# Retention and a snake feed-forward in one kernel: six 128-token tiles moved from wide TensorE tiles to 64x64 ones

## The chip, the cores and the metric

One core of a Trainium2 chip runs the kernel. The metric is the device time of one execution in microseconds (us), the median of several runs. Engines are named as in the profile: PE (TensorE, matmuls), PEld (its weight loads), DVE (VectorE), ACT (ScalarE), POOL (GpSimd), SP (SyncE). L12 is line 12 of the kernel before.

## The reference, cut to what matters

```python
# retention: B, H, S, D = 4, 8, 768, 64, token by token
state = gamma[None, :, None, None] * state + np.einsum('bhd,bhe->bhde', k[:, :, t], v[:, :, t])
y[:, :, t] = scale * np.einsum('bhd,bhde->bhe', q[:, :, t], state)
# feed-forward on x: the y of all heads side by side, [3072, 512]; w_in [512, 2048], w_out [2048, 512]
h = x @ w_in
s = np.sin(alpha * h)
g = h + s * s / (alpha + 1e-09)
return (g @ w_out).astype(np.float32)
```

## The kernel before, in words

**Tiles.** The 768 tokens of each of the 4 batches are cut into 6 tiles of 128, 24 in all, number j = 6 * batch + c. `order` (called P from L600 on) gives their sequence: P[0] to P[3] are the first tiles (c = 0) of the four batches, P[4] to P[8] are batch 0 with c = 1 to 5, P[9] and P[10] are batch 1 with c = 1 and 2, and so on. A tile's retention gives 128 columns of `xT`, the transposed input of the feed-forward. The feed-forward works on groups: group 0 is P[0] to P[3] (512 tokens), each later group g is two tiles (256 tokens; group 1 is P[4] and P[5], group 2 is P[6] and P[7]).

**Retention of a tile** has four products: scores (k times q, 128 x 128 for each head, then masked on DVE into `aT`), mix (v times `aT`), inter (the state kept from earlier tiles times q) and sums (k times v, added to the state). Inter and mix add up in PSUM, and the result, multiplied by the decay table `qg`, goes to `xT`: the tile's exit.

There are two forms. The *natural* form (`stage_A`, `stage_M`, `stage_S`, `keep_S`) holds a tile as 128 tokens on partitions. Its scores use 64-row by 128-column tiles of the PE array, its mix and sums 128-row by 64-column tiles, and its state lies as a block diagonal `s_bd`, written by ACT straight from PSUM, where the sums of a batch keep adding up in one bank (`ps`). `stage_M` issues the exit (L327, one DVE instruction) and the state copies (L303) at once. The *wide* form (`inter`, `scores`, `sums`, `mix`, gathered in `burst`) is for P[10] and later; all its matmuls are on 64x64 tiles, four of which work beside one another. A burst finishes the tile `old` while it does the scores of the tile `new`, and it returns three pieces of later work: "exit" (two DVE multiplies, L414), "keep" (two DVE adds into `s_f`, L421) and "hand" (a copy `s_q` <- `s_f`, on ACT for batches 0 to 2, L427). The phase runs these in its next slot.

**The order of the work is the program's order on each engine** (the schedule is manual). After a start with hand-written order, `phase(g, ...)` runs group g in 8 slots, (g,0) to (g,7). A slot issues, in this order: `Slot` (8 matmuls `ph`, L456, then two sines on ACT, L459), the square (L464 on ACT; in slots (1,2) and (1,5) on DVE, L466), the pieces left by the last burst (exit, keep, hand), the retention work put at this slot (`where`: P[6]'s scores at (1,1), the rest of P[6] with P[7]'s scores at (1,3), P[7] with P[8] at (1,6), then slots 1 and 5 of each phase), the mask of those scores, some `po` matmuls of the group before (L481), and `add` (two DVE instructions, L471, that end `gT` and free the `ph` bank). P[4] and P[5] are finished just before phase 1, each between `fill(4)`s, which are four `po` matmuls.

**Loads.** POOL issues all loads of q, k, v, w_in and w_out, in program order. `load_w_in(i)` is one DMA of 512 KB (four of them), L119. q, k and v of a natural tile are DMAs of 128 KB (L84).

**Tables.** `later_tables` (L193) makes `tok`, `lgq` and `expoq` on DVE, ahead of the first mask multiply.

Of the kernel before, what the change touches and what calls it, by code (L numbers as in the profile page):

```python
# [8 lines left out]
F32 = mybir.dt.float32  # L9
# [7 lines left out]
def kernel(  # L17
# [15 lines left out]
    nc = tc.nc  # L33
# [35 lines left out]

    def chunk_of(t, j):  # L70
        b, c = divmod(j, NCH)
        return t[b, :, c * C:(c + 1) * C, :].rearrange("h s d -> s h d")
# [17 lines left out]
    def spot(h):  # L90

        return h // NP, (h % NP) ^ (h // NP)

    def load_seq(bt, names="qkv"):

        cs = [c for c in range(NCH) if wide(bt * NCH + c)]
        nh = 2 * len(cs)
        if "q" in names:
            raw["seq", bt] = (big.tile([128, nh, 2, NP, D], BF16, name=f"qk_seq{bt}"),
                              big.tile([128, nh, NP, D], BF16, name=f"v_seq{bt}"))  # L100
        tqk, tv = raw["seq", bt]
        for name, src in (("q", q), ("k", k), ("v", v)):
            if name not in names:
                continue
            for h in range(H):
                b, at = spot(h)
                r = slice(64 * b, 64 * b + 64)
                o = tv[r, :, at, :] if name == "v" else tqk[r, :, "qk".index(name), at, :]
# [9 lines left out]
    def load_w_in(i):  # L118
        nc.gpsimd.dma_start(out=w_in[:, :, i * fw:(i + 1) * fw], in_=w_in_v[:, :, i * fw:(i + 1) * fw])  # L119
# [62 lines left out]
    for p in range(NP):  # L182
        for e in range(2):
            nc.vector.memset(lgp[64 * e:64 * e + 64, p:p + 1], lng[2 * p + e])
# [41 lines left out]
    s_bd = [big.tile([128, NP, 128], BF16, name=f"s_bd{i}") for i in range(2)]  # L226
# [53 lines left out]
    def stage_S(j):  # L280
        c = j % NCH
        if c == 0:
            st["ps"] = psum.tile([128, NP, D], F32, name="ps", tag="ps")
        ps = st["ps"]
        for p in range(NP):
            for e in range(2):
                nc.tensor.matmul(ps[64 * e:64 * e + 64, p, :], raw["k", j][:, 2 * p + e, :], raw["v", j][:, 2 * p + e, :],
                                 start=(c == 0 and p == 0), stop=True, skip_group_check=True)
        return ps

    def turned(to, ps, copy):

        copy(to[:, 0:2], ps[:, 0:2])
        for e in range(2):
            copy(to[64 * e:64 * e + 64, 2:4], ps[64 - 64 * e:128 - 64 * e, 2:4])

    def keep_S(j, ps):
        if wide(j + 1):
            turned(s_q[(j % NCH + 1) % 2], ps, nc.scalar.copy)
            return  # L300
        for e in range(2):
            r = slice(64 * e, 64 * e + 64)
            nc.scalar.copy(s_bd[(j % NCH + 1) % 2][r, :, r], ps[r, :, :])  # L303

    def stage_M(j):
        c = j % NCH
# [3 lines left out]
        qkT, aT, vs = st["qkT", j], st["aT", j], raw["v", j]  # L310
        py = psum.tile([128, NP, 128], F32, name="py", tag="ty")
        if c > 0:
            for p in range(NP):
                for e in range(2):
                    r = slice(64 * e, 64 * e + 64)
                    nc.tensor.matmul(py[r, p, :], s_bd[c % 2][:, p, r], qkT[:, p, :],
                                     start=(p == 0), stop=True, skip_group_check=True)
        for p in range(NP):
            for e in range(2):
                nc.tensor.matmul(py[64 * e:64 * e + 64, p, :], vs[:, 2 * p + e, :], aT[:, e, p, :],  # L320
                                 start=(c == 0 and p == 0), stop=True, skip_group_check=True)
        x = xT[g][:, :, i * C:(i + 1) * C]
        if c == 0:
            nc.scalar.copy(x, py)
            return
        ps = stage_S(j) if c < NCH - 1 else None
        nc.vector.tensor_mul(x, py, qg[:, c])  # L327
        if ps is not None:
            keep_S(j, ps)

    def half(x):
        return slice(64 * x, 64 * x + 64)
# [3 lines left out]
    def inter(j):  # L338

        qkT, s = st["qkT", j], s_q[j % NCH % 2]  # L340
        st["py", j] = [psum.tile([128, 512], F32, name=f"py{b}", tag=tag) for b, tag in enumerate(("ps", "ty"))]
        for m in range(2):
            for b, e in tiles4:
                last = nc.tensor.matmul(st["py", j][b][half(e ^ b), m * 128:(m + 1) * 128].rearrange("p (f i) -> p f i", f=2),  # L344
                                        s[half(e), 2 * b + m, :], qkT[half(e), m:m + 5:4, half(b)],
                                        start=(m == 0), stop=True, skip_group_check=True)
        return last

    def scores(j):

        qkT = st["qkT", j]
        pa = st["pa", j] = psum.tile([128, 2, 512], F32, name="pa", tag="pa")
        for m in range(2):
# [8 lines left out]
        aT = work.tile([128, 2, 2, 192], BF16, name="aTw", tag="aT", bufs=2)  # L362
        st["aT", j] = aT
# [3 lines left out]
    def sums(now, to, lo):  # L367

        ks, vs = raw["k", now], raw["v", now]
        for f in range(2 if wide(now) else 1):  # L370
            for m in range(2):
                for b, e in tiles4:
                    h = 4 * b + 2 * m + (e ^ b)
# [5 lines left out]
    def mix(j, behind):  # L379

        n = nc.tensor.nop()
        tc.add_manual_dep(n.ins, behind.ins.name, AFTER)
# [7 lines left out]

    def burst(old, new, first=None):

        c = old % NCH
        behind = inter(old)
        more = scores(new) if new is not None else {}
        now = old if c < NCH - 1 else first
        at = None
        if now is old:
# [3 lines left out]
        mix(old, behind)  # L402
        py = st["py", old]
        if now is not None and now is not old:
            at = [py[b][:, 256:384] for b in range(2)]
            sums(now, py, 256)
        g, i = place[old]
        if g not in xT:
            xT[g] = work.tile([128, KS, sizes[g] * C], BF16, name="xT", tag="xT", bufs=3)
        x = xT[g][:, :, i * C:(i + 1) * C]  # L410
# [6 lines left out]
        def keep():  # L417
            for b in range(2):
                o, add = s_f[:, 2 * b:2 * b + 2], at[b].rearrange("p (m d) -> p m d", m=2)
                if wide(now):  # L420
# [179 lines left out]
    def A(j):  # L600
        return lambda: stage_A(j)

    def M(j):
        return lambda: stage_M(j)

    def SK(j):
        return lambda: keep_S(j, stage_S(j))

# [21 lines left out]
    for t in s_bd:  # L630
        nc.vector.memset(t, 0.0)
# [58 lines left out]
    stage_A(P[4])  # L690
# [59 lines left out]
    def into_sum():  # L750
        turned(s_f, st["ps"], nc.vector.tensor_copy)

    def M_last(j):
        stage_M(j)
        into_sum()

# [55 lines left out]
```

## Time and profile before

| | |
|---|---|
| median of 3 runs | 213.49 us (213.29 to 213.51) |
| the profiled execution, its own time | 213.53 us |
| its span (first to last instruction) | 211.7 us |
| PE busy, DVE busy, ACT busy, POOL busy | 94%, 74%, 74%, 50% of the span |
| granted TensorE clock | 1.0 |
| 735 `ph` and 344 `po` matmuls, busy | 98.6 and 90.4 us |

Times in the views are us from the span's start. A row of the timeline or the chain has the start, the length, the engine, the tile or instruction with its line, and how many instructions it merges; in brackets stands how long the engine was idle before and what released it. Rows of PE give start to modelled end, so a matmul's end is later than the start of the next one; a few per cent of its records are missing (344 `po` matmuls are recorded, 368 weight loads for them).

### The profile page before, as it was taken

Reading aid. Unit: us, or ns where it says so; the run is one execution under the profiler, and the core shown is the slowest. Engines: PE = TensorE matmul, PEld = TensorE weight load, DVE = VectorE, ACT = ScalarE, POOL = GpSimd, SP = SyncE. Lnnn points to the kernel's source line nnn. Section 1 sums busy time; section 2 is a strip of 40 time slices with the busy share of each in tenths; the row PEclk is TensorE's granted clock in tenths of the full one; section 3 lists DMA queues with packets and bytes.
Section 4 is the critical chain, followed back from the end, with each engine's and each line's share of the span. In section 5 each row is a group of like instructions: output and inputs, shape, how many; then the busy total and the mean of one; then the engine's idle time right before and its main releaser. Section 6 shows DMA issues by size and latency. Waiting matters only on the chain.

```text
span 211.7 us, 5581 instructions
## 1 busy us (share of the span) xinstructions
PE 199.4 (94%) x2227; PEld 131.0 (62%) x2253; DVE 155.7 (74%) x353; ACT 157.7 (74%) x339; POOL 105.2 (50%) x140
## 2 busy tenths in 40 slices
PE   7798899899989999999999999999999999999994
PEld 3345454457766766766666667666666666666653
DVE  5877849966997688687777787777777878666550
ACT  7588696858887887877867877876876786788821
POOL 8975434977989649699799951001021020000000
PEclk9999999999999999999999999999999999999999
DMA  8999999999997989999999994403513110110112
GB/s 124 154 198 186 206 207 173 154 148 240 142 152 71 166 129 159 113 133 140 140 182 167 193 127 104 99 24 79 88 38 81 54 48 5 50 50 3 50 50 99
DMA packets 101337, 25.00 MB, mean 118 GB/s; under 512 B 93872, under 2 KB 98368, under 8 KB 101312
## 3 DMA queue, kind: packets, MB, share of 16 engines
q0 software_dynamic: 77504, 13.38, 86.7%
q1 hardware_dynamic: 23664, 11.22, 26.3%
q8 instruction: 17, 0.28, 0.6%
q14 instruction: 8, 0.07, 0.1%
q10 hardware_dynamic: 144, 0.07, 0.1%
HBM read 27.27 MB, written 6.29 MB: 159 GB/s over the span
## 4 chain that ended last, share of the span: by engine, by line
PE 78%; DVE 14%; ACT 4%; issue 3%; ACTq 0%
PE po L481 33%; PE ph L456 31%; DVE gT L471 5%; DVE aT L277 4%; PE spare L525 3%; ACT s L459 2%; ACT s L464 2%; PE poh L506 2%; PE py L344 2%; PE py L387 1%; DVE s L466 1%; PE pa L273 1%; PE pa L355 1%; PE py L320 1%; PE pa L374 1%
## 5 line engine op out<-in xcount | busy, mean ns | idle before, releaser
L471 DVE SCALAR_TENSOR_TENSOR gT<-s,rec_alpha,ph 128x256 bf16<-128x256 f32 (+3 forms) x184 | 82.4, 489 | 36.0 <-ACT s L464 35.8
L459 ACT ACTIVATE s<-ph,alpha_sb 128x256 f32<-128x256 f32 (+3 forms) x184 | 79.3, 480 | 35.2 <-PE ph L456 34.5
L456 PE MATMUL ph<-xT,w_in 128*128 128x256 bf16 (+3 forms) x735 | 98.6, 277 | 0.3 <-DVE gT L471 0.2
L481 PE MATMUL po<-w_out,gT 128*128 128x512 bf16 x344 | 90.4, 379 | 4.8 <-issue 3.3
L456 PEld LDWEIGHTS <-w_in 128*128 128x128 bf16 x736 | 70.6, 98 | 30.6 <-issue 1.0
L464 ACT ACTIVATE s<-s 128x512 f32<-128x512 f32 (+1 forms) x92 | 57.1, 621 | 2.5
L481 PEld LDWEIGHTS <-gT 128*128 128x128 bf16 x368 | 33.8, 98 | 27.7 <-issue 1.2
L427 POOL CAST s_q<-s_f 128x256 bf16<-128x256 f32 x5 | 2.0, 397 | 43.3 <-DVE s_f L421 25.7
L143 POOL TENSOR_TENSOR v_seq<-v_seq,kgq 128x512 bf16<-128x512 bf16 x14 | 14.6, 1066 | 8.8 <-ACT s L459 4.9
L109 POOL DMA_DIRECT2D qk_seq<-in_q_dram x24 | 17.1, 743 | 3.2 <-DMA v_seq<-in_v_dram 1.7
L109 POOL DMA_DIRECT2D qk_seq<-in_k_dram x24 | 17.0, 731 | 2.4 <-DMA qk_seq<-in_q_dram 1.3
L109 POOL DMA_DIRECT2D v_seq<-in_v_dram x24 | 17.0, 756 | 0.0
L493 DVE COPY o_sb<-po 128x512 f32<-128x512 f32 x19 | 13.1, 692 | 5.2 <-PE po L481 5.2
L364 DVE TENSOR_TENSOR aTw<-pa,maskq 128x768 bf16<-128x768 f32 x14 | 13.3, 952 | 0.0
L84 POOL DMA_DIRECT2D vr<-in_v_dram x10 | 9.2, 924 | 3.3 <-DMA w_in<-in_moe_w_in_dram 1.7
L525 PE MATMUL spare<-warm 128*128 128x512 bf16 x27 | 9.2, 464 | 1.3 <-DVE warm L162 1.2
L414 DVE TENSOR_TENSOR xT<-py,qg 128x256 bf16<-128x256 f32 x28 | 10.5, 417 | 0.0
L84 POOL DMA_DIRECT2D qkr<-in_q_dram x9 | 8.1, 902 | 3.8 <-DMA w_in<-in_moe_w_in_dram 1.7
L84 POOL DMA_DIRECT2D qkr<-in_k_dram x9 | 8.1, 898 | 3.9 <-DMA w_out<-in_moe_w_out_dram 3.4
L143 POOL TENSOR_TENSOR vr<-vr,kg 128x512 bf16<-128x512 bf16 x7 | 7.4, 1072 | 1.4 <-DMA vr<-in_v_dram 1.4
L277 DVE TENSOR_TENSOR aT<-pa,mask 128x1024 bf16<-128x1024 f32 x6 | 7.3, 1218 | 0.4 <-PE pa L273 0.4
L277 DVE TENSOR_TENSOR aT<-pa,dec 128x1024 bf16<-128x1024 f32 x4 | 4.9, 1223 | 1.8 <-PE pa L273 1.8
(94 smaller groups left out, 141.5 us busy)
## 6 DMA issues: line engine op xcount, KB each, us to landing
out_dram<-o_sb SPq DMA_DIRECT2D x23, 256.0 KB, 2.8
w_in<-in_moe_w_in_dram POOLq DMA_DIRECT2D x4, 512.0 KB, 11.0
w_out<-in_moe_w_out_dram POOLq DMA_DIRECT2D x4, 512.0 KB, 14.8
vr<-in_v_dram POOLq DMA_DIRECT2D x10, 128.0 KB, 6.9
qk_seq<-in_q_dram POOLq DMA_DIRECT2D x16, 80.0 KB, 6.9
qk_seq<-in_k_dram POOLq DMA_DIRECT2D x16, 80.0 KB, 5.1
v_seq<-in_v_dram POOLq DMA_DIRECT2D x16, 80.0 KB, 5.5
qkr<-in_q_dram POOLq DMA_DIRECT2D x9, 128.0 KB, 7.0
```

What stands on the lines that cost most here:

```text
L84: nc.gpsimd.dma_start(out=t, in_=chunk_of(src, j))
L109: nc.gpsimd.dma_start(out=o, in_=src[bt, h, cs[0] * C:, :].rearrange("(f i) d -> i f d", i=64))
L143: eng.tensor_mul(t, t, by[:, j % NCH, :, None].to_broadcast([128, H, D]))
L277: nc.vector.tensor_mul(aT.rearrange("p e n t -> p (e n) t"), pa.rearrange("p e n t -> p (e n) t"), m)
L364: return {"mask": lambda: nc.vector.tensor_mul(aT, pa[:, :, 0:384].rearrange("p e (m t) -> p e m t", m=2), maskq[:, None, None, :].to_broa ...
L456: nc.tensor.matmul(self.ph[:, m, :], w_in[:, i, f * 128:(f + 1) * 128], xT[g][:, i, self.lo:self.hi], start=(m == 0 and i == 0), stop=(i = ...
L459: nc.scalar.activation(out=self.s[:, m, :], in_=self.ph[:, m, :], func=ACTF.Sin, scale=alpha_sb[:, f:f + 1])
L464: nc.scalar.activation(out=self.s, in_=self.s, func=ACTF.Square)
L471: nc.vector.scalar_tensor_tensor(gT[self.g][:, f, self.lo:self.hi], self.s[:, m, :], rec_alpha[:, f:f + 1], self.ph[:, m, :], op0=ALU.mult ...
L481: nc.tensor.matmul(po[g, ts], gT[g][:, f, ts * C:(ts + 1) * C], w_out[:, f, :], start=(f == 0), stop=(f == FF - 1))
L493: nc.vector.tensor_copy(o_sb, po[g, ts])
L525: nc.tensor.matmul(spare["ps"], warm[:, :128], warm, start=True, stop=True)
```

## The change

P[4] to P[9] now go through `scores`, `inter` and `burst` as the wide tiles do, with branches for their natural layout. `s_bd`, its two memsets, `stage_S`, `keep_S`, `turned` and `into_sum` are gone.

- *Scores* of such a tile: 16 matmuls on 64x64 tiles, 128 columns each, in place of 8 on 64x128 tiles. The mask multiply keeps its size.
- *Mix and sums* come in two rounds by token half (`round_of`). In a round each of the four 64x64 tiles takes one half of the tokens: 8 matmuls of mix (4 with 128 columns, 4 with 64) and 8 of sums (64 columns). Both rounds add into the same PSUM places from different halves of the array's rows, so a `nop` on PE waits, after the next tile's scores, until the first round has ended (`behind`).
- *State*: `first_state` copies the first tile's sums to `s_q[1]` (ACT) and `s_f` (DVE); after that keep and hand do it, as in the wide form. Exit, keep and hand are run in the next slot; after P[4] and P[5] they are run at once.
- *Layout*: heads 4 to 7 no longer lie swapped in `load_seq`, in the tables (`lgq` in one copy for each half instead of two, `lgp`) and in `stage_M`'s output; instead w_in's last 256 rows are loaded with their 64-row halves swapped, as three DMAs (256, 128 and 128 KB) for each `load_w_in`.

```diff
 def load_w_in(i):
-    nc.gpsimd.dma_start(out=w_in[:, :, i * fw:(i + 1) * fw], in_=w_in_v[:, :, i * fw:(i + 1) * fw])
+    c = slice(i * fw, (i + 1) * fw)
+    nc.gpsimd.dma_start(out=w_in[:, 0:2, c], in_=w_in_v[:, 0:2, c])
+    for e in range(2):
+        nc.gpsimd.dma_start(out=w_in[half(e), 2:4, c], in_=w_in_v[half(1 - e), 2:4, c])
...
-            for e in range(2):
-                nc.vector.tensor_copy(lgq[r, e::2], lg[r, NP * b + (e ^ b):NP * b + NP:2])
+            nc.vector.tensor_copy(lgq[r], lg[r, NP * b:NP * b + NP])
...
+    def first_state(j):
+        ps = psum.tile([128, NP, D], F32, name="ps", tag="ps")
+        for p in range(NP):
+            for e in range(2):
+                nc.tensor.matmul(ps[half(e), p, :], raw["k", j][:, 2 * p + e, :], raw["v", j][:, 2 * p + e, :],
+                                 start=(p == 0), stop=True, skip_group_check=True)
+        nc.scalar.copy(s_q[1], ps)
+        nc.vector.tensor_copy(s_f, ps)
...
 def scores(j):
+        if not wide(j):
+            for p in range(NP):
+                for f, e in tiles4:
+                    nc.tensor.matmul(pa[half(f), e, 128 * p:128 * p + 128], qkT[half(e), NP + p, half(f)],
+                                     qkT[half(e), p, :], start=(p == 0), stop=True, skip_group_check=True)
...
+    def round_of(j, now, n):
+        py, aT, vs = st["py", j], st["aT", j], raw["v", j]
+        for m in range(2):
+            for b, e in tiles4:
+                f, p = e ^ n, 2 * b + m
+                last = nc.tensor.matmul(py[b][half(e ^ b), m * 128 + 64 * f:(m + 1) * 128], vs[half(f), 2 * p + e, :],
+                                        aT[half(f), e, p, 64 * f:], start=False, stop=True, skip_group_check=True)
+        if now is not None:
+            ks, vs = raw["k", now], raw["v", now]
+            for m in range(2):
+                for b, e in tiles4:
+                    f, h = e ^ b ^ n, 4 * b + 2 * m + e
+                    last = nc.tensor.matmul(py[b][half(e), 256 + 64 * m:320 + 64 * m], ks[half(f), h, :],
+                                            vs[half(f), h, :], start=False, stop=True, skip_group_check=True)
+        return last
 def burst(old, new, first=None):
-        behind = inter(old)
+        now = old if c < NCH - 1 else first
+        last = inter(old)
+        if not wide(old):
+            last = round_of(old, now, 0)
         more = scores(new) if new is not None else {}
...
+        behind(last)
...
+            round_of(old, now, 1)
...
-    stage_A(P[5])
+    scores(P[5])["mask"]()
     fill(2)
-    SK(e0)()
+    first_state(e0)
     scale_v(P[5], nc.vector)
     fill(4)
-    stage_M(P[4])
+    run(burst(P[4], None), "exit", "keep", "hand")
     fill(4)
-    stage_M(P[5])
+    run(burst(P[5], None), "exit", "keep", "hand")
     fill(4)
     where = {6: (1, 1), 7: (1, 3), 8: (1, 6)}
...
-        if n > 6 and wide(P[n - 1]):
+        if n > 6:
             at(where[n], B(P[n - 1], new, first))
         else:
-            if n > 6:
-                at(where[n], lambda j=P[n - 1], last=wide(new): (M_last if last else stage_M)(j))
-            at(where[n], lambda j=new: (scores if wide(j) else stage_A)(j))
-            if first is not None:
-                at(where[n], SK(first))
+            at(where[n], lambda j=new: scores(j))
```

More of the change, by code (lines that the diff above doesn't have):

```diff
@@ L278, in stage_A, with x_of @@
         st["aT", j] = aT
[L280 to L284, printed above, removed]
+    def first_state(j):
+        ps = psum.tile([128, NP, D], F32, name="ps", tag="ps")
         for p in range(NP):
             for e in range(2):
[L287 to L306, printed above, removed]
+                nc.tensor.matmul(ps[half(e), p, :], raw["k", j][:, 2 * p + e, :], raw["v", j][:, 2 * p + e, :],
+                                 start=(p == 0), stop=True, skip_group_check=True)
+        nc.scalar.copy(s_q[1], ps)
+        nc.vector.tensor_copy(s_f, ps)
+    def x_of(j):
         g, i = place[j]
@@ L309, in stage_M @@
             xT[g] = work.tile([128, KS, sizes[g] * C], BF16, name="xT", tag="xT", bufs=3)
-        qkT, aT, vs = st["qkT", j], st["aT", j], raw["v", j]
+        return xT[g][:, :, i * C:(i + 1) * C]
+    def stage_M(j):
+        aT, vs = st["aT", j], raw["v", j]
         py = psum.tile([128, NP, 128], F32, name="py", tag="ty")
[L312 to L317, printed above, removed]
         for p in range(NP):
             for e in range(2):
[L320 to L334, printed above, removed]
+                nc.tensor.matmul(py[half(e ^ (p // 2)), p, :], vs[:, 2 * p + e, :], aT[:, e, p, :],
+                                 start=(p == 0), stop=True, skip_group_check=True)
+        nc.scalar.copy(x_of(j), py)
     tiles4 = [(b, e) for b in range(2) for e in range(2)]
@@ L343, in inter @@
             for b, e in tiles4:
-                last = nc.tensor.matmul(st["py", j][b][half(e ^ b), m * 128:(m + 1) * 128].rearrange("p (f i) -> p f i", f=2),
-                                        s[half(e), 2 * b + m, :], qkT[half(e), m:m + 5:4, half(b)],
-                                        start=(m == 0), stop=True, skip_group_check=True)
+                o, p = st["py", j][b][half(e ^ b), m * 128:(m + 1) * 128], 2 * b + m
+                if wide(j):
+                    o, to = o.rearrange("p (f i) -> p f i", f=2), qkT[half(e), m:m + 5:4, half(b)]
+                else:
+                    to = qkT[half(e), p, :]
+                last = nc.tensor.matmul(o, s[half(e), p, :], to, start=(m == 0), stop=True, skip_group_check=True)
         return last
@@ L401, in burst @@
             sums(now, [pa[:, b] for b in range(2)], 384)
[L402 to L410, printed above, removed]
+        behind(last)
+        if wide(old):
+            mix(old)
+            if now is not None and now is not old:
+                sums(now, py, 256)
+        else:
+            round_of(old, now, 1)
+        x = x_of(old)
         def leave():
@@ L689 @@
     F((0, 1), (12,))
-    stage_A(P[4])
+    scores(P[4])["mask"]()
     a.sq("A").add()
```

46 lines of the change are left out of this document (17 added, 29 removed).

## The prediction

> **What bounds the kernel now.** I read the page first (busy shares, the chain by line), then the chain in order of time, then the timelines of PE, DVE and ACT around the six tiles, then the landings of POOL's DMAs one by one.
>
> ```profile
> PE 199.4 (94%) x2227; PEld 131.0 (62%) x2253; DVE 155.7 (74%) x353; ACT 157.7 (74%) x339; POOL 105.2 (50%) x140
> PE 78%; DVE 14%; ACT 4%; issue 3%; ACTq 0%
> ```
>
> PE bounds most of the span, but the chain's 14% of DVE is not spread out: it lies ahead of 63 us, where the changed tiles are. The chain in order of time, end of phase 1:
>
> ```profile
> 49.62 0.69 DVE qkT L259
> 50.31 0.43 DVE qg L220
> 50.74 0.09 issue
> 50.83 0.86 DVE gT L471 x2
> ...
> 59.67 0.87 DVE gT L471 x2
> 60.55 0.60 DVE xT L327
> 61.15 1.13 DVE aT L277
> 62.28 0.79 DVE gT L471 x2
> 63.07 0.04 issue
> 63.11 1.02 PE po L481 x4
> ```
>
> From 50.83 to 63.07 the chain never leaves DVE: one instruction starts as the one before ends. 60.55 is P[7]'s exit in slot (1,6), 61.15 the mask of P[8], 62.28 the add of slot 6. After 63.11 the chain is PE without a gap to the end, so what happens before it is carried to the end whole, and PE time saved after it counts in full. PE in the same stretch:
>
> ```profile
> 58.91 0.41 PE L316 MATMUL py<-qkT,s_bd 128*64 128x128 bf16 x8
> 59.16 0.39 PE L320 MATMUL py<-aT,vr 128*64 128x128 bf16 x8
> 59.38 0.29 PE L287 MATMUL ps<-vr,qkr 128*64 128x64 bf16 x8
> 59.60 0.40 PE L273 MATMUL pa<-qkT 64*128 64x128 bf16 x8
> 61.68 1.04 PE L456 MATMUL ph<-xT,w_in 128*128 128x256 bf16 x8
> 63.11 1.02 PE L481 MATMUL po<-w_out,gT 128*128 128x512 bf16 x4 [0.40 <-DVE gT L471]
> 63.97 1.04 PE L456 MATMUL ph<-xT,w_in 128*128 128x256 bf16 x8
> ```
>
> 61.68 is slot (2,0): it needs xT of P[7], ready at 61.15. 63.97 is slot (2,1). PE is only 0.56 us ahead of DVE (its 8 `ph` end at 62.55, `po` starts at 63.11).
>
> **The change, part by part.** All against the profiled execution, 213.53 us (span 211.7 and 1.83 around it), 0.04 above the median.
>
> *PE work of a burst.* Groups of four 64x64 matmuls share their time in a wide burst: inter 81.17 to 81.31, 16 scores to 81.48, 16 sums (64 columns) to 81.61, then the mix and on to `po` at 81.89 (the first recorded `po`, 82.11, less one unrecorded of 0.22). So a group costs some 0.053 us at 128 columns, 0.03 at 64. A natural burst then needs inter 0.14, a round 0.16 (0.107 mix, 0.054 sums), scores 0.21 (16 x 128 columns, as long as today's 8 at two abreast), a round and the end 0.28, and 0.10 ahead of it as now: 0.89. Today P[8] with P[9]'s scores and the sums of tile 6 in slot (2,1) takes 64.84 to 66.09, 1.25; P[9] in (2,5) 73.03 to 74.13, 1.10, against 0.88 after. Those lie after 63 us: **-0.58**. The wait of `behind` is covered where scores stand between (0.21 against a matmul's 0.19 and 0.03 of signal). The bursts in (1,3) and (1,6) also save 0.2 each, in a stretch that DVE sets: nothing.
> The Trainium skill (TensorEngine Tiling (Array Packing), Key Properties) says that a change of tiling mode drains TensorE; here the rows of sums and scores (59.38, 59.60) follow at their plain rate, so no price shows. At the 0.1 us in front of a burst for one mode fewer, the two bursts would save 0.2 more.
>
> *P[4] and P[5].* Today ACT copies the state straight from PSUM beside four `po` (45.68 to 46.44) and P[5] starts at 46.53. After the change: burst of P[4] at 44.87 (first_state's DVE copy, between the 0.28 of 128 columns and the 0.69 of 512, is done by 44.8), inter and round 0 to 45.17, an uncovered wait to 45.4, last mix ends 45.7. Then exit, keep and hand follow one another. Their rows in the wide form:
>
> ```profile
> 83.61 0.75 DVE L414 TENSOR_TENSOR xT<-py,qg 128x256 bf16<-128x256 f32 x2
> 84.27 0.47 DVE L421 TENSOR_TENSOR s_f<-s_f,pa 128x128 f32<-128x128 f32 x2
> ```
>
> That is 1.13 from 45.74, to 46.87, then 0.39 of ACT (L427) to 47.3, then P[5]'s inter at 47.38: **+0.85**, PE idle behind four `po` that end by 46.5. P[5]'s burst costs 0.1 more than today's `stage_M` (the uncovered wait), so slot (1,0) starts at 49.05 instead of 48.10. ACT's queue makes it worse: hand (49.4 to 49.8) now stands ahead of the o_sb copy (0.58) and the first sine, which waited for nothing but PE; sine at 50.35 instead of 49.18, so the first add comes at **52.0** instead of 50.83. Bounds: 0 (if the hand-off hid behind `po`) to +1.5.
>
> *DVE in phase 1.* From the first add to P[7]'s old place, 50.83 to 60.55, DVE is packed for 9.72 us. P[6]'s exit of 0.60 becomes exit and keep, 1.06 back to back: 10.18.
>
> *P[7]'s exit moves behind two things.* Today it stands ahead of P[8]'s mask; as a left-over piece it runs in slot (1,7), behind that mask (1.13) and the add of slot 6 (0.79), and takes 0.75: 52.0 + 10.18 + 1.13 + 0.79 + 0.75 = 64.85. Slot (2,0) needs it: 64.9 instead of 61.68. Its `ph` (0.87) and the four `po` (0.86; their wait of 0.56 is gone, that add being done) bring slot (2,1) to 66.63 instead of 63.97: **+2.66**. Hand of P[6] on ACT holds up the sines of slot 5 to 60.35, just ahead of the DVE square that needs them (60.5): nothing more.
>
> *Tables.* Two of four small copies (L201) go. The chain runs through them: tables from 7.10, first mask multiply at 8.70, ten instructions in 1.60 us: 0.16 each, **-0.3**. Bounds 0 and -1.0 (two recorded durations of 0.49). What follows has cover of 0.35 from the landings (w_in's first piece lands at 15.0, used at 15.57). The memsets of s_bd (0.55 at 17.35) lie ahead of 0.60 of DVE idle: nothing.
>
> *Loads.* Eight more DMAs, some 0.75 us each on POOL: 6.0 us. POOL waits there anyway; each issue starts just after the eighth one before it has landed:
>
> ```profile
> 15.35 0.74 POOL L119 DMA_DIRECT2D w_in<-in_moe_w_in_dram  x1 [1.29 <-DMA w_in<-in_moe_w_in_dram]
> 17.87 0.74 POOL L122 DMA_DIRECT2D w_out<-in_moe_w_out_dram  x1 [1.78 <-DMA w_in<-in_moe_w_in_dram]
> 25.50 0.87 POOL L84 DMA_DIRECT2D qkr<-in_q_dram  x1 [1.65 <-DMA w_in<-in_moe_w_in_dram]
> ```
>
> Such waits sum to 13 us between 15 and 36. The landings are paced by bytes, not by issues (one after another 2.5 us for 512 KB, 0.9 for 128 KB, from 12.5 to 43), and with the same eight in flight I get the same landings. Nothing, unless half-height pieces are slower, below.
>
> **Sum:** 2.66 - 0.58 - 0.3 = +1.78: 213.53 + 1.78 = **215.3**.
>
> **Rivals.**
>
> *DVE follows PE (not slower).* Place: DVE from 50.83 to 63.07. If its instructions stand back to back only because PE and ACT release them at that pace, the added keeps and the late exit slip into slack, and only P[5]'s late start and PE's savings are left: 0.95 - 0.4 (the two bursts in phase 1) - 0.58 - 0.3 = -0.33, 213.2. It decides once DVE reaches P[7]'s exit 2.4 us sooner than I reckon, at PE's own arrival (61.68 + 0.95 - 0.4 = 62.2). For it: in the whole kernel DVE's adds wait 35.8 us for ACT. Against it: in this stretch the waits are 0.02 to 0.09, and PE, not DVE, waits at its end. Chance 0.14.
>
> *Half-height loads run at half rate.* Place: the 64-row pieces. Half of each w_in load at twice the time is 1.25 more, 5.0 in all; landings have little slack (P[5]'s k at 40.0, its transposes at 40.1), so nearly all comes through: 213.53 + 1.78 + 4.7 = 220.0. For it: POOL's 64-row loads of 64 KB (L109) moved one each 0.7 us, 94 GB/s, against 152 for 128-row ones. Against: that is POOL's own issue time, not the data's. Chance 0.06.
> The Trainium skill (DMA: Bandwidth & Descriptors, The descriptor swizzle) describes a 128-partition load in which half the engines write partitions 0 to 63 and half the rest, which would be this rival if a 64-row piece kept to its half; the same page's section on how many engines a DMA takes gives 64 rows all sixteen, which would be my case. No row here tells the two apart.
>
> *Otherwise* my mechanism: 0.80.
>
> **The numbers.** My own case reaches from 213.9 (no stall ahead of P[5], -0.7 for the tables) to 216.6 (the tables and the PE savings give nothing, the hand-off at its upper bound). To hold 8 in 10 the range takes in the upper half of the first rival: 213.3 to 216.7. Within 0.2% (0.43 us), about what a measurement of this kernel can tell from no change, lie some 0.10 of the first rival and 0.02 of my case; below it 0.05; slower 0.83.
>
> **What would show it.** After: PE idle some 0.9 us ahead of P[5]'s inter, released by ACT s_q; a PE idle of over 2 us ahead of the `ph` of slot (2,0), released by the DVE xT of L414's counterpart; DVE packed from 52 to 65; the natural bursts of phase 2 at 0.9 us. I am wrong if slot (2,0) starts when PE gets there, if w_in's pieces land later than 15.0, 17.6, 25.3 and 30.4, or if PE waits for DMA before 43 us.

## The result, and the profile after

The changed kernel takes **216.45 us** (median of 4 runs, 215.85 to 217.34) against 213.44 us of the kernel before: a ratio of 1.0145, 95% interval 1.0106 to 1.0184. It is slower, as forecast; the time lies 1.15 us above the forecast of 215.3 and inside its range. The profiled execution is one of the long ones: 217.34 us, span 215.6.

The page of the changed kernel, its busy shares, its row of the granted clock in 40 slices, and the chain by engine:

```profile
PE 201.2 (93%) x2371; PEld 130.8 (61%) x2397; DVE 157.6 (73%) x365; ACT 155.2 (72%) x331; POOL 110.4 (51%) x148
PEclk9999999999996999999999999999999999999999
PE 72%; DMA 12%; DVE 7%; POOL 5%; issue 2%; ACT 0%; POOLq 0%
```

PE is busy for longer though its bursts got shorter: one slice, about 65 to 70 us, ran at a lower clock. DMA and POOL are on the chain now; before, it held neither. The chain in order of time around the late exit:

```profile
52.15 0.87 DVE gT L475 x2
...
61.44 0.87 DVE gT L475 x2
62.32 1.13 DVE aT L334
63.45 0.49 DVE gT L475 x2
63.94 0.20 issue
64.14 0.43 DVE xT L418
64.58 0.04 issue
64.62 1.15 PE ph L460 x8
```

L475 is the add (L471 before), L334 the mask, L418 the exit. From the first add at 52.15, DVE is packed for 10.17 us up to P[8]'s mask (62.32); then come the mask, the add of slot 6 and P[7]'s exit, and slot (2,0) starts when the first half of that exit has ended. PE's timeline there (in brackets its idle time before, and the releaser):

```profile
64.62 1.15 PE L460 MATMUL ph<-xT,w_in 128*128 128x256 bf16 x8 [1.85 <-DVE xT L418]
...
66.98 1.91 PE L460 MATMUL ph<-xT,w_in 128*128 128x256 bf16 x8
```

The first row is slot (2,0), the second slot (2,1). Its eight matmuls take 1.91 us instead of 1.04. Busy times in stretches of 2 us say why; the number after POOL's count is the granted clock:

```profile
62.00:64.00 2.00, 0.77 (x6) 0.34 (x4) 2.00 (x4) 1.47 (x3) 1.06 (x2) 1.00 3.07 151
64.00:66.00 2.00, 1.38 (x10) 0.97 (x10) 2.00 (x7) 0.68 (x2) 1.40 (x3) 0.98 2.39 115
66.00:68.00 2.00, 2.00 (x8) 1.03 (x7) 0.42 (x2) 1.58 (x4) 2.00 (x3) 0.50 0.64 41
68.00:70.00 2.00, 1.97 (x61) 1.42 (x60) 0.71 (x3) 1.04 (x3) 2.00 (x4) 0.66 0.27 55
```

PE has little to do while it waits for DVE (0.77 and 1.38 of 2 us), and then runs at half clock from about 65.9 to 69.3. Nothing in the prediction counted that.

The starts of the feed-forward slots (first matmul of L460, in the profiled execution of each kernel; the forecast's are those that it names, without its -0.3 for the tables; its (2,2) and (2,6) are its (2,1) with the distances of before less the savings that it forecast for the bursts) show where the time goes. From (2,6) on nothing changes: each difference there stands unchanged at the last slot (199.88 before, 203.57 after: 3.69 both times).

| slot | before | forecast | after | exit_first | exit_add_mask | keep_first | hand_later | v_ahead |
|---|---|---|---|---|---|---|---|---|
| (1,0) | 48.10 | 49.05 | 49.34 | 50.22 | 48.93 | 49.56 | 48.57 | 49.07 |
| (1,7) | 60.38 | - | 61.30 | 62.17 | 60.90 | 61.52 | 60.83 | 61.02 |
| (2,0) | 61.68 | 64.9 | 64.62 | 63.57 | 62.39 | 64.84 | 62.33 | 62.44 |
| (2,1) | 63.97 | 66.63 | 66.98 | 67.13 | 65.95 | 66.68 | 64.30 | 64.41 |
| (2,2) | 66.96 | 69.26 | 70.78 | 69.82 | 68.65 | 69.38 | 68.71 | 67.55 |
| (2,6) | 75.00 | 77.08 | 78.69 | 77.73 | 76.56 | 77.29 | 76.61 | 75.46 |

### The profile page after: what moved, and what is told of

It reads as the page before. It is cut to its first block, busy times and chain, and to the rows that moved or that the text cites. A ratio compares the mean times of both kernels' runs of the same rounds, so it can differ in the third digit from the quotient of the medians.

```text
span 215.6 us, 5863 instructions
## 1 busy us (share of the span) xinstructions
PE 201.2 (93%) x2371; PEld 130.8 (61%) x2397; DVE 157.6 (73%) x365; ACT 155.2 (72%) x331; POOL 110.4 (51%) x148
## 4 chain that ended last, share of the span: by engine, by line
PE 72%; DMA 12%; DVE 7%; POOL 5%; issue 2%; ACT 0%; POOLq 0%
PE po L485 32%; PE ph L460 30%; DMA w_in<-in_moe_w_in_dram 7%; DMA qkr<-in_k_dram 5%; DVE gT L475 3%; PE py L321 2%; POOL qkr L87 2%; POOL vr L87 2%; PE poh L510 2%; DVE aT L334 2%; PE py L372 1%; DVE xT L418 1%; PE pa L338 1%; PE pt L253 1%; POOL w_out L123 1%
## 5 line engine op out<-in xcount | busy, mean ns | idle before, releaser
L475 DVE SCALAR_TENSOR_TENSOR gT<-s,rec_alpha,ph 128x256 bf16<-128x256 f32 (+3 forms) x184 | 82.5, 489 | 37.5 <-ACT s L468 37.2
L460 PE MATMUL ph<-xT,w_in 128*128 128x256 bf16 (+3 forms) x735 | 99.9, 279 | 2.6 <-DVE xT L418 1.9
L460 PEld LDWEIGHTS <-w_in 128*128 128x128 bf16 x736 | 70.8, 98 | 34.3 <-issue 4.0
L144 POOL TENSOR_TENSOR v_seq<-v_seq,kgq 128x512 bf16<-128x512 bf16 x14 | 14.6, 1065 | 9.8 <-issue 6.2
L418 DVE TENSOR_TENSOR xT<-py,qg 128x256 bf16<-128x256 f32 x40 | 15.0, 418 | 1.9 <-PE py L389 1.9
L431 ACT CAST s_q<-s_f 128x256 bf16<-128x256 f32 x14 | 5.5, 392 | 6.8 <-DVE s_f L425 6.8
L334 DVE TENSOR_TENSOR aT<-pa,mask 128x1024 bf16<-128x1024 f32 x6 | 7.3, 1222 | 1.9 <-PE pa L331 1.7
L144 POOL TENSOR_TENSOR vr<-vr,kg 128x512 bf16<-128x512 bf16 x7 | 8.0, 1153 | 1.3 <-DMA vr<-in_v_dram 1.3
```

The lines of the kernel that those rows point to most:

```text
L144: eng.tensor_mul(t, t, by[:, j % NCH, :, None].to_broadcast([128, H, D]))
L334: return {"mask": lambda: nc.vector.tensor_mul(aT.rearrange("p e n t -> p (e n) t"), pa.rearrange("p e (n t) -> p (e n) t", n=NP), mask_bc)}
L418: nc.vector.tensor_mul(x[:, 2 * b:2 * b + 2, :], py[b][:, 0:256].rearrange("p (m t) -> p m t", m=2), qg[:, c, 2 * b:2 * b + 2])
L460: nc.tensor.matmul(self.ph[:, m, :], w_in[:, i, f * 128:(f + 1) * 128], xT[g][:, i, self.lo:self.hi], start=(m == 0 and i == 0), stop=(i = ...
L475: nc.vector.scalar_tensor_tensor(gT[self.g][:, f, self.lo:self.hi], self.s[:, m, :], rec_alpha[:, f:f + 1], self.ph[:, m, :], op0=ALU.mult ...
```

## The experiments

The theory: P[7]'s exit, queued on DVE behind P[8]'s mask and the add of slot 6, costs most of it, and P[4]'s exit ahead of its hand-off most of the rest. The rivals: the loads in pieces, and the clock. From one re-ordering to the next the intervals of the ratio overlap, so what a single step does is read from its trace. L numbers from here on are of the changed kernel; "before" on the same chips was 213.48 or 213.49.

**again** and **again2**: the changed kernel, two more times.

> The changed kernel once more, beside the others. Theory: the median comes near 216.3 us; where the granted clock is 1.0 throughout, slot (2,1) starts some 2.4 us later than before (63.97), and the execution takes 215.7 to 216.2; where the clock falls behind the idle time ahead of slot (2,0) it takes 1 to 1.5 us more, so the runs of this kernel scatter over 1 us or more. Rival (the scatter is not of the clock): every run has a clock of 1.0 and they scatter as much.

Measured: 217.35 us (215.76 to 217.69), ratio 1.0161, 1.0122 to 1.0200. The profile repeats the wait: slot (2,0) at 65.05 after 1.90 idle. It also shows one reason why executions of this kernel differ. DVE scales P[5]'s v while POOL scales P[6]'s (both L144). The rows of the first measurement, then those of again:

```profile
44.88 1.60 POOL L144 TENSOR_TENSOR vr<-vr,kg 128x512 bf16<-128x512 bf16 x1 [1.32 <-DMA vr<-in_v_dram]
44.89 0.68 DVE L144 TENSOR_TENSOR vr<-vr,kg 128x512 bf16<-128x512 bf16 x1
```

```profile
44.86 1.04 POOL L144 TENSOR_TENSOR vr<-vr,kg 128x512 bf16<-128x512 bf16 x1 [1.32 <-DMA vr<-in_v_dram]
44.91 1.55 DVE L144 TENSOR_TENSOR vr<-vr,kg 128x512 bf16<-128x512 bf16 x1
```

In every trace of a changed kernel one of the two is long: 1.59 or 1.60 on POOL (1.04 otherwise), or up to 1.56 on DVE (0.68 otherwise). P[4]'s exit, keep and hand stand on DVE and ACT behind DVE's row. So P[5]'s inter comes 2.59 us after P[4]'s where DVE's row is short, and 2.92 to 2.96 where it takes 1.51 to 1.55 (again, again2, exit_first, pe_filled). Before the change rows of 0.96 and 1.38 (before, before_half) made no difference: 1.66 both times.

> The changed kernel a third time, on the chip of pe_filled, to have its executions at a clock of 0.992 counted there: 4 of 10 have shown one, so 2 to 4 of some 6, and a median of 216.3 to 217.4. If none shows one, pe_filled tells nothing of the clock.

Measured: 216.40 us (215.54 to 218.47), ratio 1.0116, 1.0096 to 1.0136. (The expectation miscounts: 5 executions, not 4, of the first 10 had shown a mean clock of 0.991 or 0.992.) The count missed as well: again2 showed one such execution in 6, where 2 to 4 were expected. In all, 6 of 16 did (1 of 4, 4 of 6 and 1 of 6); they average 217.64 us, the other ten 216.23. So a fall of the clock costs some 1.4 us, and the schedule without it costs 2.7.

**exit_first**: in slot (1,6), the exit of P[7] ahead of P[8]'s mask.

```diff
+            if (g, n) == (1, 6):
+                run(fresh, "exit")
             run(fresh, "mask")
```

> In slot (1,6) alone the exit of P[7] is issued before the mask of P[8], as it was before the change. Theory (the late exit holds up slot (2,0), but the add of slot 6, which frees a bank for the po matmuls, is the next limit): slot (2,0) starts at 63.0 instead of 64.6, slot (2,1) only some 0.5 us earlier, since the add of slot 6 now ends at 64.9; TensorE's longest idle is cut in two pieces, so the clock stays at 1.0 and the median falls by 0.5 to 1.2 us against the changed kernel. Rival (the exit alone is the price): slot (2,1) starts 1.5 us or more earlier.

Measured: 215.66 us (215.09 to 217.87), ratio 1.0113, 1.0069 to 1.0156; no execution below a clock of 0.997. PE's timeline:

```profile
63.57 1.15 PE L460 MATMUL ph<-xT,w_in 128*128 128x256 bf16 x8
65.81 1.02 PE L485 MATMUL po<-w_out,gT 128*128 128x512 bf16 x4 [1.09 <-DVE gT L475]
67.13 1.03 PE L460 MATMUL ph<-xT,w_in 128*128 128x256 bf16 x8 [0.29 <-ACT o_sb L499]
```

The wait ahead of slot (2,0) is gone, although this execution began phase 1 late (slot (1,0) at 50.22). But the `po` behind it now wait 1.09 for the add of slot 6, which the mask still holds up, and slot (2,1) waits for ACT. From (1,0) to (2,1) it takes 16.91 us, against 15.87 before. The changed kernel's 17.64 is no fair measure, since its clock fell ahead of (2,1); keep_first and w_whole below hold the same late exit and take 17.12 at full clock. So this step regains some 0.2 of 1.25: the wait has mostly moved.

**exit_add_mask**: exit, add and only then the mask.

```diff
+            late = {}
+            if (g, n) == (1, 6):
+                run(fresh, "exit")
+                late["mask"] = fresh.pop("mask")
             run(fresh, "mask")
...
             now.add()
+            run(late, "mask")
```

> In slot (1,6) alone VectorE's order is exit of P[7], add of slot 6, mask of P[8]; the mask is wanted only in slot (2,1). Theory: slot (2,0) at 63.0, the po matmuls behind it at 63.9 without a wait, slot (2,1) at 64.8 instead of 66.3 (at full clock): 1.5 us less than the changed kernel at full clock, 1.5 to 2.3 us in the median with the clock at 1.0, near 214.2. Rival (VectorE's backlog, not the order, is what counts): the mask only moves the wait to slot (2,1) and less than 0.5 us is won.

Measured: 215.69 us (214.99 to 216.78), ratio 1.0100, 1.0063 to 1.0137, all clocks 0.998 or more. No median gain over exit_first: slot (2,0) and its `po` (63.51) now wait less than 0.2 each, but the next slot waits 1.42. PE's row and, after it, ACT's:

```profile
65.95 1.03 PE L460 MATMUL ph<-xT,w_in 128*128 128x256 bf16 x8 [1.42 <-ACT o_sb L499]
```

```profile
65.01 0.41 ACT L431 CAST s_q<-s_f 128x256 bf16<-128x256 f32 x1 [1.53 <-DVE s_f L425]
65.32 0.58 ACT L499 COPY o_sb<-po 128x512 f32<-128x512 f32 x1
```

Slot (2,1) needs a PSUM bank that the `o_sb` copy frees. On ACT that copy stands behind the hand of P[7], which waits for keep on DVE, and keep stands behind the mask. From (1,0) to (2,1) it takes 17.02, 0.1 less than 17.12. So the rival came true: the mask only moved the wait to slot (2,1), by way of ACT.

**hand_later**: exit_add_mask, and P[7]'s hand one slot later, behind that copy.

```diff
-            run(more, "exit", "keep", "hand")
+            run(more, "exit", "keep")
+            if (g, n) != (1, 7):
+                run(more, "hand")
```

> As the kernel with the order exit, add, mask in slot (1,6), and the hand of P[7] put off from slot (1,7) to slot (2,0), behind the o_sb copy, the sines and the square on ScalarE. Theory (in the former run slot (2,1) waited 1.4 us for that o_sb copy, which stood behind the hand): the wait goes, slot (2,1) starts 2.1 to 2.3 us after slot (2,0) instead of 3.6, and the median falls by 1.0 to 1.5 us more, to 214.2 to 214.7. Rival (the copy is late for another reason, or the next limit stands close behind): less than 0.5 us.

Measured: 215.08 us (214.68 to 216.87), ratio 1.0094, 1.0066 to 1.0122. The step itself held: slot (2,1) follows (2,0) after 1.97 us (3.56 in exit_add_mask) without a wait. From (1,0) to (2,1) it takes 15.73, so the whole 1.25 is regained: it was the order on DVE's and ACT's queues together. Yet the median gains only 0.6 where 1.0 to 1.5 were expected, because PE then meets something new. PE's timeline in the burst of slot (2,1), and after it POOL's:

```profile
65.63 0.31 PE L321 MATMUL py<-qkT,s_q 64*64 64x128 bf16 x8 [0.29 <-ACT s_q L431]
66.22 0.30 PE L382 MATMUL py<-aT,vr 64*64 64x128 bf16 x8 [0.28 <-POOL vr L144]
67.21 0.26 PE L389 MATMUL py<-vr,qkr 64*64 64x64 bf16 x8 [0.69 <-POOL vr L144]
```

```profile
63.63 1.47 POOL L107 DMA_DIRECT2D qk_seq<-in_k_dram  x2 [0.87 <-DMA vr<-in_v_dram]
65.11 3.04 POOL L144 TENSOR_TENSOR vr<-vr,kg 128x512 bf16<-128x512 bf16 x3
```

POOL scales the values of P[8] and of e1, the first tile of the next batch (L144, one us each), and they stand on its queue behind eight loads of k, the last of which wait for earlier loads to land. They start at 65.11; the kernel before started them at 62.55, the changed one at 65.58. There PE was too late to notice.

**v_ahead**: hand_later, and those two multiplications earlier on POOL's queue (`load_seq` calls `mid` after six of its eight DMAs).

```diff
     scale_v(P[7], nc.gpsimd)
+    scale_v(e1, nc.gpsimd)
     load_chunk(P[9], "v")
-    load_seq(1, "k")
-    scale_v(P[8], nc.gpsimd)
-    scale_v(e1, nc.gpsimd)
+    load_seq(1, "k", mid=lambda: scale_v(P[8], nc.gpsimd))
     scale_v(P[9], nc.gpsimd)
```

> hand_later, and on POOL's queue the scaling of P[8]'s v moved ahead of the last two of the eight loads of k for sequence 1, and that of e1's v moved up behind that of P[7]'s; the same instructions, two of them earlier. In hand_later's trace PE reaches P[8]'s inter at 65.63 and then waits 0.28 and 0.69 us for POOL's two multiplications (L144, 65.11 to 67.14), which stand behind eight issues of loads, each of which waits for an earlier load to land. Theory that this queue is the limit that follows: both waits go, slot (2,2) starts at about 67.75 in place of 68.71, and the median falls by 0.9 to 1.0 us, to 214.1 (214.0 to 214.3), with the wait for s_q (0.29) still there. Rival, that P[8]'s v lands too late for it (it was seen to land between 61.8 and 64): POOL then waits for that landing ahead of the last loads of k, PE waits for the same multiplication at about the same time, and the median stays at 215.0 to 215.3 or rises.

Measured: 214.57 us (214.08 to 215.49), ratio 1.0061, 1.0041 to 1.0082. Slot (2,2) at 67.55, 1.2 us sooner; both waits for `vr` are gone:

```profile
63.07 1.04 POOL L146 TENSOR_TENSOR vr<-vr,kg 128x512 bf16<-128x512 bf16 x1 [0.27 <-DMA vr<-in_v_dram]
```

The profiled execution (214.20) came where the theory put it; the median gained 0.5 where 0.9 to 1.0 were expected, so half of that is not accounted for (one execution of this kernel differs from the next by up to 1.4 us). It is the best version that was run, the first whose interval lies below all three of the changed kernel, and still slower than before.

**keep_first**: the changed kernel, P[4]'s keep and hand ahead of its exit.

```diff
-    run(burst(P[4], None), "exit", "keep", "hand")
+    run(burst(P[4], None), "keep", "hand", "exit")
```

> The changed kernel with keep and hand of P[4] issued ahead of its exit, nothing else. Theory (P[5]'s first matmul waits for exit, keep and hand in a row): hand ends 0.7 us earlier, P[5]'s inter then waits for the exit alone and comes 0.3 to 0.4 us earlier (0.9 behind the po matmuls today, 0.5 then), and 0.3 to 0.4 us are won at an equal clock and equal landings. Rival (the wait is of the uncovered first round or of the banks): no gain.

Measured: 215.98 us (215.44 to 218.01), ratio 1.0145, 1.0110 to 1.0179.

```profile
47.62 0.53 PE L321 MATMUL py<-qkT,s_q 64*64 64x128 bf16 x8 [0.40 <-ACT s_q L431]
```

P[5]'s inter comes 2.29 us after P[4]'s (45.33). DVE's row of L144 was a long one here (1.53), so the runs to compare are those with such a row, 2.92 to 2.96: 0.63 to 0.67 earlier (0.30 against the 2.59 with a short row). From P[5]'s scores to slot (2,0) it takes 21.64, against 22.13 in again. The ratio's interval covers that of the changed kernel, so the step shows in the trace and not in the median. Slot (2,0) still waits 1.85 for the late exit. No execution fell to 0.992, though this one holds the same idle stretch.

**v_keep**: v_ahead and keep_first together.

> v_ahead, and P[4]'s keep and hand ahead of its exit as in keep_first. Theory that the limits are independent: P[5]'s inter comes 0.3 us earlier, slot (1,0) too, and the median is 0.2 to 0.4 us under v_ahead's, 213.7 to 213.9: within 0.2 per cent of the kernel before. Rival, that PE's earlier start only meets the next data later in phase 1 (P[7]'s hand at 59.5, the transpose of P[8] at 61, P[8]'s v): within 0.2 us of v_ahead, or above it.

Measured: 214.70 us (213.67 to 215.36), ratio 1.0057, 1.0037 to 1.0078: no gain, which is the rival's number. P[5]'s inter waits 0.43 instead of 0.70, and slot (1,0) starts 0.29 sooner than in v_ahead. Then P[7]'s inter waits 0.36 for its hand at 59.87, and slot (1,7) is 0.15 later than in v_ahead. But in this trace DVE's square of slot (1,2) (L472, at 54.30) takes 1.20 us, 0.68 in v_ahead, and that alone is more than the lead. So whether the later data would have eaten it without that row is not shown.

**best**: hand_later, keep_first, and P[5]'s hand put off into slot (1,0).

> All of it together: exit, add, mask in slot (1,6), hand of P[7] in slot (2,0), keep and hand ahead of the exit for P[4], and P[5]'s hand put off to slot (1,0) behind the o_sb copy and the first sines. Theory: what the change costs at P[5] falls from 0.95 + 0.2 to 0.6 us, the late exit costs nothing, and the tables and the shorter bursts give 0.9: between 0 and 0.6 us less than the kernel before, where w_in lands in time; with late landings up to 0.5 above it. Rival (some wait that I have not seen follows the ones removed): 214 or more.

Measured: 217.97 us (216.89 to 219.50), ratio 1.0218, 1.0187 to 1.0248: a miss, no faster than the change itself. In its trace slot (2,1) starts at 65.14, but (2,2) at 70.32, 5.2 us later. Between them P[8]'s inter waits 0.67 for s_q, then PE twice 0.69 for POOL's multiplications (from 66.72, the latest of all runs); ahead of that, its scores had waited for a transpose:

```profile
61.08 0.42 PE L331 MATMUL pa<-qkT 64*64 64x128 bf16 x16 [0.49 <-DMA qkT<-qkr]
```

PE is busy for only 1.35 of the 3.4 us from 66.0, and 4 of 6 executions show a clock of 0.991 or 0.992. It leaves the order on POOL's queue as it was. The wait ahead of slot (2,0) is gone here (63.34), and the clock falls all the same.

**w_whole**: the changed kernel with w_in in whole 512 KB loads; it leaves out the swap of the 64-row halves.

```diff
-        nc.gpsimd.dma_start(out=w_in[:, 0:2, c], in_=w_in_v[:, 0:2, c])
-        for e in range(2):
-            nc.gpsimd.dma_start(out=w_in[half(e), 2:4, c], in_=w_in_v[half(1 - e), 2:4, c])
+        nc.gpsimd.dma_start(out=w_in[:, :, c], in_=w_in_v[:, :, c])
```

> The changed kernel with each load of w_in in one DMA as before, so that the 64-row halves of w_in's last 256 rows are not swapped: heads 4 to 7 meet the wrong weights, all else is as it was. Theory (the three pieces delay the stream of loads by 1 us, at the first two loads only): P[4]'s k lands at 37.2 or before instead of 38.3, TensorE no longer waits for w_in's first piece nor for the k of e3 and P[4], the scores of P[5] start at 42.0 to 42.3 instead of 42.9, and 0.6 to 0.9 us are won. Rival (the loads are hidden, as predicted): the same landings or the same start of P[5]'s scores, and no gain.

Measured: 217.70 us (216.18 to 218.71), ratio 1.0196, 1.0150 to 1.0241; three of six executions at a clock of 0.991 or 0.992. Nothing comes back, so the pieces are not what makes most of the change slow. Its first w_in load landed at 16.4 even as one DMA (15.0 before):

```profile
16.40 3.42 PE L457 MATMUL ph<-xT,w_in 128*128 128x384 bf16 x20 [0.86 <-DMA w_in<-in_moe_w_in_dram]
```

**before_half**: the kernel before, with w_in in the three pieces, halves not swapped.

```diff
+        for r in (slice(0, 64), slice(64, 128)):
+            nc.gpsimd.dma_start(out=w_in[r, 2:4, c], in_=w_in_v[r, 2:4, c])
```

> The kernel before with each load of w_in in the three pieces of the change (256 KB and two of 64 rows), the halves not swapped. Theory (the loads are hidden, as predicted; the late landings in some executions come with one DMA in three as well): within 0.3 us of the kernel before, w_in's first load complete at 14.5 to 15.5. Rival (the pieces delay the stream by 1 us): P[4]'s k lands at 38.2 or later instead of 37.2 and the median rises by 0.4 to 0.8 us. Second rival (64-row pieces at half rate): w_in's loads take 1.2 us longer each, 4 us or more in all.

Measured: 213.85 us (213.45 to 214.81, 12 runs), ratio 1.0024, 1.0008 to 1.0040. The four loads were complete at 15.0, 17.9, 25.3 and 30.5, so two 64-row pieces side by side move at the full rate; what remains is 0.36 us. POOL's multiplications of P[8] start at 63.42 here, 0.87 later than before. Yet the profiled execution (214.36) does not show the loads at work: slot (1,0) starts at 48.05, not later than before (48.10). What makes it 0.83 longer is one row on DVE, the square of slot (1,2) (at 53.49), which takes 1.57 us where before it took 0.69. Whether the 0.36 us of the medians come from the loads is therefore not shown.

**pe_filled**: the changed kernel with work for PE in the wait ahead of slot (2,0).

```diff
+            if (g, n) == (2, 0):
+                pw = psum.tile([128, 2, 512], F32, name="pw", tag="pa")
+                for _ in range(4):
+                    nc.tensor.matmul(pw[:, 0], warm[:, :128], warm, start=True, stop=True)
```

> The changed kernel, and ahead of slot (2,0)'s first matmul four matmuls of 128x512 on a tile of zeros into the bank of the scores, read by nobody: more work on PE, nothing taken away. They can start when P[8]'s mask has read that bank (some 63.5 us) and end before xT is there (64.6), so they cost no time by themselves and leave PE idle for about 0.8 us in place of 1.85. Theory that PE's idle stretch is what lets the granted clock fall: no execution at a clock of 0.992, and a median of 216.0 to 216.4, the mean of the changed kernel's executions without a fall, though the kernel does more. Rival, that something else in the late schedule lets it fall (DVE's packed stretch, the burst of small matmuls): executions at 0.992 as often as in the changed kernel, and a median no lower than its 216.4 to 217.4.

Measured: 216.03 us (215.97 to 216.75, 4 runs), ratio 1.0125, 1.0108 to 1.0141, all clocks 0.998 or more. PE's timeline, and the busy times after it:

```profile
63.81 1.02 PE L589 MATMUL pw<-warm 128*128 128x512 bf16 x4 [0.82 <-DVE aT L334]
64.93 1.15 PE L460 MATMUL ph<-xT,w_in 128*128 128x256 bf16 x8
```

```profile
66.00:68.00 2.00, 2.00 (x35) 1.25 (x37) 0.42 (x2) 1.97 (x6) 2.00 (x3) 1.00 0.42 26
```

Slot (2,0) starts as late as in the changed kernel, and (2,1) 1.84 later, at full clock. The median is what the theory said, but its interval overlaps that of again2. And 0 falls in 4 against 6 in 16 could be chance (a 15% one), all the more against the 1 in 6 of again2 on the same chip.

Taken together the runs say more. Look in each trace for the 3.4 us in which PE is busy least, from 9 to 75 us. In after, again, again2, keep_first, w_whole and best that is 1.36 to 1.55 us, and 13 of these kernels' 34 executions show a clock of 0.991 or 0.992. In exit_first, exit_add_mask, hand_later, v_ahead, v_keep and pe_filled it is 1.89 us or more, and none of 34 does. Among the first, best has its poorest stretch after slot (2,0). So a stretch with little work for PE goes with the falls, wherever it lies; where there was more work for it, none was seen. One trace stands for all executions of a kernel here, and keep_first, with 1.54 us, shows none in 6.

## Why the prediction was right, and where it was off

**The late exit of P[7]: right.** Forecast: first add at 52.0, DVE packed for 10.18, slot (2,0) at 64.9, slot (2,1) at 66.63. Measured: 52.15, 10.17, 64.62 and 66.98; without a fall of the clock (keep_first) 64.84 and 66.68. That it is the order on DVE's queue which holds up (2,0) is shown by exit_first and exit_add_mask, which move nothing else and start it with a wait under 0.2. What is lost at (2,1) hangs on more than the exit's own place: those two regain 0.2 and 0.1 of 1.25, and only hand_later, which also moves the hand on ACT, regains all. The idle stretch was 1.85 instead of "over 2 us", since PE needs only the first half of the exit.

**P[5]'s start: right in kind, too small in size.** Inter at 47.61 after 0.70 idle on s_q (forecast 47.38, "some 0.9"). From P[5]'s scores to slot (1,0) it takes 6.44 us against 5.31: +1.13, for the forecast's +0.95; in again and again2, with the long row of L144 on DVE, +1.50 and +1.48. keep_first and v_keep took 0.3 to 0.67 off the way from P[4]'s inter to P[5]'s and nothing that shows off the median.

**Two phase 2 bursts, -0.58: right in kind, smaller.** From (2,1) to (2,2) keep_first takes 2.70 and the kernel before 2.99: -0.29 for the forecast's -0.36. From (2,2) to (2,6) the changed kernel takes 7.91 against 8.04: -0.13 for -0.22. Together -0.42. In the profiled execution of the changed kernel the first became +0.81, at half clock.

**The price of a change of tile shape: misread.** The prediction took it from the rows at 59.38 and 59.60 that no price shows. But there eight sums of 64 columns are followed by the scores after 0.22 us, as long as eight mix matmuls with twice the columns take (59.16 to 59.38, no change of shape). The same mix in slot (2,1) of the kernel before, followed by scores on another shape, shows it better:

```profile
65.19 0.39 PE L320 MATMUL py<-aT,vr 128*64 128x128 bf16 x8
65.51 0.40 PE L273 MATMUL pa<-qkT 64*128 64x128 bf16 x8
```

That is 0.32 instead of 0.22, and from these scores to the sums at 65.84 it is 0.33: a change of shape costs some 0.10 us here, as it does in front of a burst. The Trainium skill (TensorEngine Tiling (Array Packing), Key Properties) says that such a change drains TensorE, and the trace agrees. The burst of (2,1) went from four changes to two and that of (2,5) from three to two, so some 0.3 of the 0.42 saved is this (an estimate from the 0.10). It does not come on top of the -0.58: that sum compares whole rows of before, with their changes in them, against a burst that has only the two.

**Tables -0.3 right, loads "nothing" wrong.** Ten table instructions in 1.60 us became eight in 1.30 (6.65 to 7.95). But P[5]'s scores start at 42.90 against 42.79. The step that failed is "with the same eight in flight I get the same landings": the first w_in load was complete at 16.0 (15.0 forecast), and PE waited for DMA before 43 us, which the prediction had named as a sign of being wrong:

```profile
38.34 0.40 PE L253 MATMUL pt<-ident,qkr 128*128 128x128 bf16 x4 [0.37 <-DMA qkr<-in_k_dram]
```

The pieces alone do not make the loads late: in before_half they were complete at 15.0, 17.9, 25.3 and 30.5, as whole loads are, and the medians differ by 0.36 us (0.2 to 0.9 by the interval of the ratio). The lateness comes and goes between executions (in hand_later's the same load was complete at 15.1, in w_whole's unsplit one at 16.4) and its cause stays open. The loads also reach further than the landings that the prediction listed: POOL's multiplications for P[8] stand in the same queue, which only hand_later made visible.

**The clock: not in the sum.** It is most of the distance between 215.3 and the 217.34 of the profiled execution: 1.4 in the executions that have it. How the other terms close is seen in keep_first's profiled execution, which holds the same idle stretch and no fall: 215.81, 0.51 above the forecast. Of that, 0.30 are the tables' gain that never reached P[5]'s scores, 0.05 slot (2,1) (66.68 for 66.63) and 0.16 the bursts (-0.42 for -0.58). That the 0.05 is so small is partly luck: slot (1,0) came 0.51 later than forecast (49.56 for 49.05), and the way from there to (2,1) was 0.46 shorter (17.12 for 17.58), most of it because PE did not wait for the second half of the exit. The changed kernel's ten executions without a fall average 216.23, another 0.4 more; they differ by up to 1.7 among themselves. DVE's row of L144, short or long, is one reason (0.33 to 0.37 at P[5]'s inter); the landings below are a likely other that no run isolates.

**The rivals.** "DVE follows PE" (213.2) is out: PE waited 1.85 us for DVE. Half-rate loads (220.0) are out by before_half. That does not decide between the two sections of the Trainium skill (DMA: Bandwidth & Descriptors; The descriptor swizzle, and Why a DMA increments its semaphore by 16 and not by 1, where it says how many engines a DMA takes): the two 64-row pieces of a load are in flight together, so half the engines for each would show the same rate.

## What to carry to other kernels

When leftover pieces of a tile are put off to the next slot, read what the engine's queue holds between the old place and the new one; here one mask and one add, 1.9 us, decided, with the hand and the copy that queued behind them. When one such wait is removed, look for the next engine with its work in a fixed order: four stood here behind one another (DVE's mask, DVE's add, ACT's hand ahead of a copy that frees a bank, POOL's multiplications behind loads), and the three re-orderings that put the pieces elsewhere returned 1.9 of 3.0 us (216.45 to 214.57), a part of it by ending the falls of the clock. Count the changes of tile shape in a burst, too: each took 0.10 us. A stretch in which PE mostly waits can cost a second time, through the clock, after it is over.

## What the runs showed of the hardware that was not expected

The granted clock fell to 0.5 although PE never stood idle for more than 1.9 us. In the three profiled executions with a fall (after, again, again2) it lasted from 65.93 to 69.34, from 65.88 to 69.29 and from 66.64 to 70.05, worked out from the granted clock in stretches of 0.2 us: 3.41 us each time. In the 3.4 us before it PE was busy for 1.50 to 1.55 us (45%). The profiled executions of keep_first, w_whole and best have as little in such a stretch, 1.54, 1.55 and 1.36 us, and no fall. The Trainium skill (TensorE: Matmul & The Clock Gate, The HAM clock gate) gives a window of about 3.4 us that runs free of the program, and that fits the length and why only some executions show it. It lets the clock fall after an idle window; here a window in which PE was 45% busy was enough.

DVE and POOL rows of one and the same multiplication (L144) that start within 0.1 us of each other do not both run at their short length: one took 0.68 and the other 1.60, or 1.55 and 1.04. The rows do not say why. Only in the changed kernel does PE wait for what stands behind DVE's row.

Landings of loads differ by about 1 us between executions that issue them alike: the first w_in load was complete at 16.0 in after and 15.1 in hand_later, and as one whole DMA at 15.0 in before and 16.4 in w_whole. Executions of the kernel before range from 212.7 to 215.1 us. What starts that was not found.
